# Gated MLP behind windowed attention on one core: 128 queries scored as two halves with 192 keys each, one tile for both heads' last blocks, P transposed by row halves

## The chip, the cores and the metric

The kernel runs on 1 core of one Trainium2 chip. The metric is device time in microseconds (us) of one execution. TensorE (PE; its weight loads are PEld), VectorE (DVE), ScalarE (ACT), GpSimd (POOL) and SyncE (SP) each work through their own queue in order and wait for one another by semaphores.

## The reference

There are 8 batches, 8 heads, 576 positions and a head size of 64. Attention looks back over a window of 128 positions, with a bias that falls with distance; a gated MLP follows, with a layer norm and a product along the sequence.

```python
scores = scale * np.matmul(q, k.transpose(0, 1, 3, 2))
slopes = 2.0 ** (-8.0 * (np.arange(H, dtype=np.float32) + 1) / H)
bias = slopes[:, None, None] * (-np.abs(rel).astype(np.float32))[None, :, :]
mask = (rel >= 0) & (rel < window)
scores = np.where(mask, scores + bias[None], -1000000000.0)
attn = np.exp(scores - np.max(scores, axis=-1, keepdims=True))
attn = attn / (np.sum(attn, axis=-1, keepdims=True) + 1e-09)
x = np.matmul(attn, v)                       # then heads side by side: (8, 576, 512)

h = np.maximum(x @ w_in, 0.0)                # 512 -> 1024
u, v = h[..., :512], h[..., 512:]
v_n = (v - mu) / np.sqrt(var + 1e-06)        # mean and variance over the 512
v_s = np.einsum('ts,bsd->btd', w_spatial, v_n) + b_spatial[None, :, None]
out = (u * v_s) @ w_out                      # 512 -> 512
```

## The kernel before

**Who sets the order.** Every step is handed to a planner (`Plan`) with its engine, an estimated cost, a due time and the buffers it reads and writes. `order` plays these through a list schedule (the ready step with the earliest due time goes first on its engine) and the steps are then written out in that order. Each engine's queue is therefore fixed at build time; semaphores enforce the data dependences at run time. `plan.buf(pool, tag, n, ...)` takes the next of `n` buffers that a tag cycles through, and a step on it depends on the users of the buffer that it replaces.

**The MLP.** For each batch `gated` runs five units on `v` (four `v_unit`, L711, and the remainder `v_rem`, L733), then eight `u_unit` (L763), eight `sp_unit` along the sequence (L784) and eight `o_unit` (L810). Every operand is kept as a high and a low part and multiplied in three passes, so a unit has 12 matmuls, `sp_unit` 14 and `v_rem` 8.

**Attention in the score way.** Heads go in pairs: there are four pairs (b, p) per batch. `scores` loads q, k and v, and `products` computes S = QK as 64-query blocks with at most 192 keys each (L527). The 64x64 products of both heads and both query halves are written into PSUM tiles of 128 queries by up to 256 keys. A tile t holds queries 128 t to 128 t + 127 and keys from 128 (t - 1) to the end of its queries, for one head: 128 columns for t = 0, 256 for t = 1 to 3, and 192 columns on 64 rows for t = 4. That is ten tiles per pair. Where a 64-query block does not reach, the table adds a large negative number. Tiles 0 to 3 of the two heads lie in the four banks tagged `s`; tile 4 of each head lies in the last 192 columns of the two banks x0 and x1 (tag `y`). For each tile VectorE adds the bias table and takes the minimum (L538), ScalarE takes exp and the row sum (L544), and after the sums' reciprocals ScalarE writes the scaled high part as fp16 into `pq` (L579) and VectorE the low part (L584). One DMA transpose per head turns all 18 blocks of 128 columns of `pq` into `pt` (L590), which has three half-pair buffers.

`attention` follows one pair later (`AHEAD = 1`). It scales and splits v (L602 to L633; a small DMA transpose at L613 spreads a maximum), multiplies V by the transposed P into x0 and x1, 288 queries in each (L646), and writes x with its low part (L655 on ScalarE, L659 on VectorE).

**Attention in the single-precision way.** At the start nothing else is ready, so `raw_tile` computes some pairs in plain fp32: scores (L444), table (L450), exp (L455), a transpose on TensorE (L473) and the product with v (L491). Before the change this holds for the four pairs of batch 0 and for pair (1,0). Only after that does `clear` zero the last columns of `pq` on POOL (L506).

**Preparation.** `split_w64` takes the weights, which arrive as 64-bit floats, apart into two parts. For `w_out` its staging buffers are those of `pt` and `vraw`, and the result has a place of its own.

**The queue of SP.** It issues every DMA: the loads of q and k (L423) and v (L425), the transposes (L590, L613), the weights and the stores (L820).

Of the kernel before, what the change touches and what calls it, by code (L numbers as in the profile page):

```python
# [44 lines left out]

class Plan:
# [94 lines left out]
def attn_gmlp_kernel(ctx, tc, qk, v, w_in, w_spT, b_sp, w_out, outT):  # L141
# [3 lines left out]
    nc = tc.nc  # L145
# [11 lines left out]
    VORDER = (0, 4, 1, 2, 3)  # L157

# [4 lines left out]
    WTMP, WST = ("vraw", 3), ("pt", 3)  # L163
# [21 lines left out]
    plan.kept["y"] = [x[:, 512 - 3 * D:].rearrange("p (a b) -> p a b", a=1) for x in plan.kept["x"]]  # L185
# [22 lines left out]
    ident = fixed([P, P], F32, "ident")  # L208
    powers = fixed([P, 2], F32, "powers")
    tabs = [fixed([P, 2 * P], BF16, f"tab{h}") for h in range(H)]  # L210
    win = fixed([P, NC_, 2, DF], F32R, "win")
    wout = fixed([P, ND, 2, DM], F32R, "wout")
# [4 lines left out]
    NB = 2 * NQ - 1  # L217
    OFF = [0] + [(2 * t - 1) * P for t in range(1, NQ)]
    prob = [fixed([P, NB * P], F32, f"prob{j}") for j in range(2)]
    pq = [fixed([P, 2, NB * P], F16, f"pq{j}") for j in range(2)]  # L220
    stat = [fixed([P, 4, 2, NQ], F32, f"stat{i}") for i in range(2)]
# [11 lines left out]
    maskt = plan.buf(work, "u", 7, [P, 2 * P], F32)  # L233
    minus = plan.buf(work, "u", 7, [P, P], F32R)

    def constants():
# [31 lines left out]
        for j in range(2):  # L268
            def f(j=j):
                nc.vector.memset(stat[j](), 1.0)  # L270
            plan.add("DVE", dve(64), 600, f, (), [(stat[j], x) for x in range(99)])
        for h in range(H):
            def f(h=h):
                slope = 2.0 ** (-8.0 * (h + 1) / H)
                nc.vector.scalar_tensor_tensor(tabs[h](), relf(), -8.0 * slope, maskt(), ALU.mult, ALU.add)
            plan.add("DVE", dve(256), 1000 + h * 4000, f, [(relf, 0), (maskt, 0)], [(tabs[h], 0)])
# [11 lines left out]
    def split_w64(src, dst, tmp, hi, lo, due, on_pe):  # L288
# [25 lines left out]
        copy(n, lambda: (hi(), x()), due + 3, [X], [HI], fast=True)  # L314
# [9 lines left out]
        if not on_pe:  # L324
            def f():
# [29 lines left out]
    def wout_weights(c, due):  # L355
        st = plan.buf(work, *WST, [P, DM, 2], I32)
# [4 lines left out]
        tmp = [plan.buf(work, *WTMP, [P, DM], F32) for _ in range(2)]  # L361
        split_w64((st, DM), (wout, (c,)), tmp, lambda: wout()[:, c, 0, :], lambda: wout()[:, c, 1, :], due, WPE[2])
# [67 lines left out]
    def raw_tile(b, p, t, raw, vr, xt, slot, due):  # L430
# [7 lines left out]
        pr = [lambda j=j: prob[j]()[:m, slot * 2 * P:slot * 2 * P + n] for j in range(2)]  # L438
        cols = [parts(prob[j], slot * 2 * P, slot * 2 * P + n) for j in range(2)]
# [6 lines left out]
        for j in range(2):  # L446
            h = 2 * p + j

            def f(j=j, h=h):
                nc.vector.tensor_tensor_reduce(pr[j](), sc[j]()[:m, 0, :n], tabs[h]()[:m, c0:c0 + n], -0.125, 3e38,  # L450
                                               ALU.add, ALU.min, st(NM, j))
            plan.add("DVE", dve(n), due + 300, f, [(sc[j], 0), (tabs[h], 0)], cols[j] + [(rstat, row)])
# [13 lines left out]
        tp = plan.buf(ps, *(("m", 2) if b == 0 else ("s", 4)), [P, 2, 2 * P], F32)  # L466
# [37 lines left out]
    def clear():  # L504
        for j in range(2):
            plan.add("POOL", 500, 0, lambda j=j: nc.gpsimd.memset(pq[j]()[:, :, OFF[NQ - 1]:], 0.0), (),  # L506
                     [k for a in range(2) for k in parts(pq[j], a * NB * P + OFF[NQ - 1], (a + 1) * NB * P)])


    BANKS = (((0, 1), ("s", 4)), ((2, 3), ("s", 4)), ((4,), ("y", 2)))  # L510

    WINDOWS = (((0, 0, 256, 0), (1, 256, 160, 128), (2, 512, 32, 256)),
               ((1, 416, 96, 0), (2, 544, 224, 0), (3, 768, 192, 96), (4, 1024, 64, 224)))

    def products(p, due, st, raw, RAWS, g, banks):

        SM, NM, RC, TM = range(4)
        sc = [[plan.buf(ps, *tag, [P, 2, 2 * P], F32) for _ in range(2)] for _, tag in banks]
        span = [(k, i, t, min(P, S - t * P), max(0, (t - 1) * P), min(S, (t + 1) * P)) for k, (ts_, _) in enumerate(banks) for i, t in enumerate(ts_)]

        def f():
            for k, i, t, m, k0, k1 in span:
                for q in range(t * P, t * P + m, D):
                    for j in range(2):
                        rows, out = slice(j * D, (j + 1) * D), slice(q - t * P, q - t * P + D)
                        a, z = max(k0, q - P), q + D
                        nc.tensor.matmul(sc[k][j]()[out, i, a - k0:z - k0], raw()[rows, 0, q:q + D], raw()[rows, 1, a:z],  # L527
                                         start=True, stop=True, skip_group_check=True)
        plan.add("PE", SWITCH + pe(*[4 * min(x[5] - x[4], 3 * D) for x in span]), due - 5000 + g * 3000, f, RAWS,
                 [(sc[k][j], i) for k, i, *_ in span for j in range(2)])  # L530
        for k, i, t, m, k0, k1 in span:
            for j in range(2):
                h, n, c0 = 2 * p + j, k1 - k0, P if t == 0 else 0
                pt = lambda j=j, m=m, t=t, n=n: prob[j]()[:m, OFF[t]:OFF[t] + n]
                d = due - 4500 + (t if len(banks) < 3 or t < NQ - 1 else -1) * 700 + j * 200

                def f(sc=sc[k][j], pt=pt, i=i, j=j, h=h, t=t, m=m, n=n, c0=c0):
                    nc.vector.tensor_tensor_reduce(pt(), sc()[:m, i, :n], tabs[h]()[:m, c0:c0 + n], -0.125, 3e38,  # L538
                                                   ALU.add, ALU.min, st()[:m, NM, j, t:t + 1])
                cols = parts(prob[j], OFF[t], OFF[t] + n)  # L540
                plan.add("DVE", dve(n), d, f, [(sc[k][j], i), (tabs[h], 0)], cols + [(st, (NM, j, t))])

                def f(pt=pt, j=j, t=t, m=m):
                    nc.scalar.activation(pt(), pt(), AF.Exp, bias=st()[:m, NM, j, t:t + 1], scale=-1.0,  # L544
                                         accum_out=st()[:m, SM, j, t:t + 1])
# [359 lines left out]
```

## Time and profile before

| | |
|---|---|
| time, median of three runs | 641.73 us (641.16 to 642.12) |
| span of the profiled execution | 640.1 us |
| PE busy | 598.2 us (93%), 5388 matmuls |
| PEld busy | 521.6 us (81%) |
| DVE busy | 533.7 us (83%) |
| ACT busy | 435.0 us (68%) |
| POOL busy | 30.4 us (5%) |
| DMA | 80.27 MB, 125 GB/s mean |

The profile shows one execution. Its own time is not listed apart from its span; the span runs from its first to its last instruction, and the three runs' median stands 1.6 us above it. Busy time of an engine counts overlapping instructions once. In a row of instruction groups the columns are the line of the kernel, the engine, the operation, the tiles (written <- read), their shapes, the count, then busy us, mean ns of one, and the idle time before them with the instruction that ended it. Matmuls overlap each other, so the mean of one is longer than the distance between two.

### The profile page before, as it was taken

How to read it: one execution, taken by the hardware profiler on the slowest of the kernel's cores; microseconds unless marked ns; L12 is line 12 of the kernel's file. 1: busy time of each engine (PE TensorE's matmuls, PEld its weight loads, DVE VectorE, ACT ScalarE, POOL GpSimd, SP SyncE). 2: the span in 40 equal slices, each digit the busy share in tenths (PEclk: the TensorE clock that was granted, in tenths of full speed). 3: DMA queues.
4: the chain of work that ended last, by engine and by line, in shares of the span. 5: the costliest groups of instructions: out<-in, count | busy, mean ns of one | idle time of the engine just before them, and what ended most of it. 6: DMA issues, size and time to landing. Idle time of an engine off the chain costs nothing. (4 is left out here: it accounts for less than half of the span.)

```text
span 640.1 us, 14937 instructions
## 1 busy us (share of the span) xinstructions
PE 598.2 (93%) x5388; PEld 521.6 (81%) x5388; DVE 533.7 (83%) x1953; ACT 435.0 (68%) x1324; POOL 30.4 (5%) x53
## 2 busy tenths in 40 slices
PE   4879899699999999999999999999999999999997
PEld 2445588588789978987789978998799878988997
DVE  7999898989997998889995999779979989873632
ACT  4697675897865887789762787667857987463211
POOL 1000010000100001000100001000100001000100
PEclk9997799899999999999999999999999999999999
DMA  7903123699456782498643774739567863433001
GB/s 265 335 19 99 47 67 102 145 219 183 123 135 134 142 203 54 112 187 213 142 95 80 172 171 98 120 112 200 90 129 168 151 134 65 78 73 77 0 19 57
DMA packets 153614, 80.27 MB, mean 125 GB/s; under 512 B 132930, under 2 KB 144194, under 8 KB 153540
## 3 DMA queue, kind: packets, MB, share of 16 engines
q1 hardware_dynamic: 153540, 79.32, 53.4%
q8 instruction: 42, 0.69, 0.5%
q14 instruction: 32, 0.26, 0.1%
HBM read 37.13 MB, written 9.44 MB: 73 GB/s over the span
## 5 line engine op out<-in xcount | busy, mean ns | idle before, releaser
L544 ACT ACTIVATE prob<-prob,stat 128x256 f32<-128x256 f32 (+2 forms) x270 | 126.0, 469 | 18.0 <-DVE stat L538 17.9
L784 PE MATMUL m<-wsp,vn 128*128 128x288 f32 x768 | 121.5, 297 | 2.7 <-ACT o L281 1.5
L810 PE MATMUL m<-gs,wout 128*128 128x288 f32 x768 | 111.5, 300 | 4.4 <-DVE u L792 1.6
L763 PE MATMUL m<-xt,win 128*128 128x288 f32 x768 | 112.0, 298 | 3.6 <-ACT u L285 1.8
L810 PEld LDWEIGHTS m<-gs,wout 128*128 128x128 f32 x768 | 103.5, 189 | 11.8 <-DVE u L792 2.5
L784 PEld LDWEIGHTS m<-wsp,vn 128*128 128x128 f32 x768 | 107.4, 188 | 6.2 <-ACT o L281 2.0
L763 PEld LDWEIGHTS m<-xt,win 128*128 128x128 f32 x768 | 104.0, 188 | 8.4 <-ACT u L285 3.0
L579 ACT ACTIVATE pq<-prob,stat 128x128 f16<-128x128 f32 x270 | 105.3, 467 | 4.6 <-DVE stat L567 2.0
L584 DVE SCALAR_TENSOR_TENSOR pq<-prob,stat,pq 128x128 f16<-128x128 f32 x270 | 105.8, 436 | 2.7 <-ACT pq L579 2.1
L711 PE MATMUL m<-win,xt 128*128 128x512 f32 x384 | 94.8, 400 | 3.4 <-ACT vt L285 1.9
L711 PEld LDWEIGHTS m<-win,xt 128*128 128x128 f32 x384 | 71.8, 191 | 23.9 <-ACT vt L285 4.1
L538 DVE CUSTOM_DVE_ANT_0 prob<-s,tab 128x256 f32<-128x256 f32 (+2 forms) x222 | 75.0, 380 | 0.3
L792 DVE TENSOR_TENSOR u<-m,u 128x288 f32<-128x288 f32 x64 | 28.6, 452 | 33.9 <-PE m L784 33.7
L681 POOL TENSOR_TENSOR st<-st,nhalf 128x1 f32<-128x1 f32 (+1 forms) x40 | 26.4, 660 | 553.3 <-DVE st L677 523.4
L544 ACT ACTIVATION_READ_ACCUMULATOR prob<-prob,stat 128x1 f32 (+1 forms) x270 | 51.4, 190 | 0.0
L285 ACT ACTIVATE u<-m 128x288 f32<-128x288 f32 x51 | 20.5, 406 | 45.2 <-PE m L763 45.0
L527 PE MATMUL s<-qkraw 64*64 64x192 f32 (+2 forms) x876 | 44.1, 318 | 6.8 <-DVE stat L538 6.8
L527 PEld LDWEIGHTS s<-qkraw 64*64 64x64 f32 x876 | 31.4, 136 | 13.2 <-DVE stat L538 9.7
L646 PE MATMUL x<-pt,vh 128*64 128x256 f16 (+6 forms) x756 | 41.8, 229 | 0.0
L646 PEld LDWEIGHTS <-vh 128*64 128x64 f16 x756 | 32.0, 110 | 5.6 <-issue 5.5
L281 ACT COPY o<-m 128x288 f32<-128x288 f32 x33 | 13.0, 395 | 33.8 <-PE m L810 32.2
L659 DVE SCALAR_TENSOR_TENSOR xt<-x,am,xt 128x288 fp32r<-128x288 f32 x54 | 25.6, 510 | 12.1 <-ACT xt L655 11.6
(134 smaller groups left out, 858.0 us busy)
## 6 DMA issues: line engine op xcount, KB each, us to landing
qkraw<-in_qk_dram SPq DMA_DIRECT2D x28, 576.0 KB, 4.5
out_dram<-o SPq DMA_DIRECT2D x64, 144.0 KB, 2.1
vraw<-in_v_dram SPq DMA_DIRECT2D x28, 320.0 KB, 3.0
vn<-in_w_in_dram SPq DMA_DIRECT2D x6, 512.0 KB, 6.3
pt<-in_w_out_dram SPq DMA_DIRECT2D x4, 512.0 KB, 4.1
gs<-in_w_spT_dram SPq DMA_DIRECT2D x4, 288.0 KB, 5.0
xt<-in_w_in_dram SPq DMA_DIRECT2D x2, 512.0 KB, 6.4
qkraw<-in_qk_dram SPq DMA_DIRECT2D x3, 320.0 KB, 8.6
```

The costliest lines, as they stand in the source:

```text
L527: nc.tensor.matmul(sc[k][j]()[out, i, a - k0:z - k0], raw()[rows, 0, q:q + D], raw()[rows, 1, a:z], start=True, stop=True, skip_group_chec ...
L538: nc.vector.tensor_tensor_reduce(pt(), sc()[:m, i, :n], tabs[h]()[:m, c0:c0 + n], -0.125, 3e38, ALU.add, ALU.min, st()[:m, NM, j, t:t + 1])
L544: nc.scalar.activation(pt(), pt(), AF.Exp, bias=st()[:m, NM, j, t:t + 1], scale=-1.0, accum_out=st()[:m, SM, j, t:t + 1])
L579: nc.scalar.activation(pq[j]()[:m, 0, cs], prob[j]()[:m, cs], AF.Copy, scale=st()[:m, RC, j, t:t + 1])
L584: nc.vector.scalar_tensor_tensor(pq[j]()[:m, 1, cs], prob[j]()[:m, cs], st()[:m, RC, j, t:t + 1], pq[j]()[:m, 0, cs], ALU.mult, ALU.subtract)
L646: nc.tensor.matmul(xp()[j * D:(j + 1) * D, x0:x0 + n], l()[:, kt, j * D:(j + 1) * D], rhs[:, o:o + n], start=j not in seen, stop=False, sk ...
L681: nc.gpsimd.tensor_tensor(st()[:m, 11:12], st()[:m, 10:11], nhalf()[:m], ALU.pow)
L711: nc.tensor.matmul(pt(), xt[c]()[:, X0[a] + t * P:X0[a] + (t + 1) * P], win()[:, c, w, DH:DF], start=(n == 0), stop=(n == 3 * NC_ - 1))
L763: nc.tensor.matmul(pt()[:, :HS], win()[:, c, w, d * P:(d + 1) * P], xt[c]()[:, X0[a] + hf * HS:X0[a] + (hf + 1) * HS], start=(n == 0), sto ...
L784: nc.tensor.matmul(pt()[:, :HS], l, r, start=(n == 0), stop=(n == len(ops) - 1))
L792: nc.vector.tensor_tensor(u(), pt()[:, :HS], u(), ALU.mult)
L810: nc.tensor.matmul(pt()[:, :HS], wout()[:, d, w, e * P:(e + 1) * P], gs[d]()[:, a, :], start=(n == 0), stop=(n == 3 * ND - 1))
```

## The change

Parts of the diff that only rename or pass arguments are left out.

- A score tile of 128 queries no longer spans 256 keys. Its two halves of 64 queries keep their own 192 keys in the same 192 columns, so tiles 1 to 3 have 192 columns instead of 256. The bias tables are cut to match (`tabs`), by copies from the full tables.
- The last 64 queries of both heads share one tile of 128 rows by 256 columns (`tabl` is its table), in the bank x0 alone; the two banks' other columns hold 256 and 320 queries of x instead of 288 each. Its products come first in `products`, and its tile comes last on VectorE. A pair has nine tiles.
- `prob`, `pq` and `stat` hold both heads in one buffer. In `pq` the halves lie at columns such that their keys line up when rows 0 to 63 are transposed from 64 columns further on than rows 64 to 127. So each head has two transposes of 64 rows, of 14 blocks of 128 columns for the first head and of 18 for the second, which has the shared tile. `pt` has two buffers for a whole pair.
- All of `pq` is cleared once on POOL. Pair (1,0) goes the score way; only batch 0 keeps the single-precision way, with its buffers placed in the ones that are used later (`told`, `more`, `raw3`).
- `w_out` is staged in the place where its result goes, so the high part is written after the last read of the staging.

```diff
-    WTMP, WST = ("vraw", 3), ("pt", 3)
+    WTMP = ("vraw", 3)
-    WHOLE = 2
-    RAW = {(0, p) for p in range(4)} | {(1, p) for p in range(1)}
...
-    plan.kept["y"] = [x[:, 512 - 3 * D:].rearrange("p (a b) -> p a b", a=1) for x in plan.kept["x"]]
+    plan.kept["y"] = [plan.kept["x"][0][:, 2 * P:]]
...
+    def tables():
+        plan.add("POOL", 700, 60000, lambda: nc.gpsimd.memset(tabl(), MASKED), (), [(tabl, 0), (tabl, 1)])
+        ...
+                nc.sync.dma_start(tabs()[rows], told()[rows, :, cs])
+            plan.add("SP", 800, 60000, f, heads, [(tabs, i)])
+            ...
+                nc.sync.dma_start(tabl()[rows, :, (1 - i) * D:(1 - i) * D + W], src[:, :, i, cs])
+            plan.add("SP", 800, 60000, f, heads, [(tabl, i)])
...
     def wout_weights(c, due):
-        st = plan.buf(work, *WST, [P, DM, 2], I32)
+        st = plan.buf(work, f"wout{c}", 1, [P, DM, 2], I32)
...
     def clear():
-        for j in range(2):
-            plan.add("POOL", 500, 0, lambda j=j: nc.gpsimd.memset(pq[j]()[:, :, OFF[NQ - 1]:], 0.0), (),
+        plan.add("POOL", 2500, 0, lambda: nc.gpsimd.memset(pq(), 0.0), (), parts(pq, 0, PQ, 64))
...
-    BANKS = (((0, 1), ("s", 4)), ((2, 3), ("s", 4)), ((4,), ("y", 2)))
+    def pieces(p):
+        out = []
+        for j in range(2):
+            for t in range(NQ - 1):
+                n = T0 if t == 0 else W
+                out.append((2 * j + (t == 3), (2 * W, 0, W, 0)[t], n, j * HEAD + (0 if t == 0 else T0 + (t - 1) * W),
+                            BASE[j] + (0 if t == 0 else T0 + (t - 1) * 2 * P + D), PLANE[j], lambda h=2 * p + j, n=n: tabs()[:, h, W - n:]))
+        out.append((4, 0, 2 * P, 2 * HEAD, BASE[1] + PLANE[0], PLANE[1], lambda: tabl()[:, p, :]))
+        return out
...
-            for k, i, t, m, k0, k1 in span:
-                for q in range(t * P, t * P + m, D):
+            for j in range(2):
+                one(4, (1 - j) * D, j, j, 2 * NQ - 2, (2 * NQ - 4) * D)
+            for t in range(NQ - 1):
+                for half in range(2):
                     for j in range(2):
-                        rows, out = slice(j * D, (j + 1) * D), slice(q - t * P, q - t * P + D)
-                        a, z = max(k0, q - P), q + D
-                        nc.tensor.matmul(sc[k][j]()[out, i, a - k0:z - k0], raw()[rows, 0, q:q + D], raw()[rows, 1, a:z],
-                                         start=True, stop=True, skip_group_check=True)
+                        i = 2 * t + half
+                        one(tiles[j * (NQ - 1) + t][0], tiles[j * (NQ - 1) + t][1], j, half, i, (i - 2) * D + (D if t == 0 else 0))
...
-            pts.append(plan.buf(work, "pt", 3, [P, 2 * NB, P], F16))
-                nc.sync.dma_start_transpose(out=pts[j](), in_=pq[j]().rearrange("p a b -> p (a b)"))
-            plan.add("SP", 3400, d + 1500, f, parts(pq[j], 0, 2 * NB * P), [(pts[j], 0)])
+            nb = 2 * PLANE[j] // P
+            for half in range(2):
+                c0 = BASE[j] + (1 - half) * D
+                ...
+                    rows = slice(half * D, (half + 1) * D)
+                    nc.sync.dma_start_transpose(out=pts()[:, BLOCK[j]:BLOCK[j] + nb, rows], in_=pq()[rows, c0:c0 + nb * P])
+                plan.add("SP", 1700, d + 1500 + half, f, parts(pq, c0, c0 + nb * P, 64), [(pts, (j, half))])
...
-            qs = slice(hf * HS, (hf + 1) * HS)
+            q0, q1 = (0, QSPLIT) if hf == 0 else (QSPLIT, S)
```

More of the change, by code (lines that the diff above doesn't have):

```diff
@@ L72, in either @@
         deps, starts = set(), set()
+        reads, writes = ([(b.of, (b.key, part)) if isinstance(b, Sub) else (b, part) for b, part in x] for x in (reads, writes))
         for b, part in reads:
@@ L207, in attn_gmlp_kernel @@
     nhalf = fixed([P, 1], F32, "nhalf")
-    ident = fixed([P, P], F32, "ident")
     powers = fixed([P, 2], F32, "powers")
-    tabs = [fixed([P, 2 * P], BF16, f"tab{h}") for h in range(H)]
+    tabs = fixed([P, H, W], BF16, "tabs")
+    tabl = fixed([P, NP, 2 * P], BF16, "tabl")
     win = fixed([P, NC_, 2, DF], F32R, "win")
-    wout = fixed([P, ND, 2, DM], F32R, "wout")
+    wout = {}
     wsp = fixed([P, NQ - 1, 2, S], F32R, "wsp")
@@ L216, in attn_gmlp_kernel @@
     l2 = fixed([P, DH], F32R, "l2")
[L217 to L221, printed above, removed]
+    NT = 2 * (NQ - 1) + 1
+    prob = fixed([P, 2 * HEAD + 2 * P], F32, "prob")
+    PLANE = [7 * P, 9 * P]
+    BASE = [0, 2 * PLANE[0] + D]
+    BLOCK = [0, 14]
+    PQ = BASE[1] + 2 * PLANE[1] + D
+    pq = fixed([P, PQ], F16, "pq")
+    stat = [fixed([P, 4, NT], F32, f"stat{i}") for i in range(2)]
     rstat = fixed([P, 8, 8], F32, "rstat")
@@ L233, in attn_gmlp_kernel @@
     maskt = plan.buf(work, "u", 7, [P, 2 * P], F32)
+    ident = plan.buf(work, "u", 7, [P, P], F32)
     minus = plan.buf(work, "u", 7, [P, P], F32R)
+    pt_raw, pt_tab = (plan.buf(work, "pt", 2, [P, 2048], F32) for _ in range(2))
+    raw3 = Sub(pt_raw, "raw", lambda x: x[:, :2 * S].rearrange("p (a s) -> p a s", a=2))
+    vr3 = Sub(pt_raw, "v", lambda x: x[:, 2 * S:2 * S + NQ * P].rearrange("p (t n) -> p t n", t=NQ))
+    told = Sub(pt_tab, "tab", lambda x: x[:, :H * P].bitcast(BF16).rearrange("p (h n) -> p h n", h=H))
+    more = Sub(pt_tab, "prob", lambda x: x[:, H * P:H * P + 4 * P])
     def constants():
@@ L413, in tail, with load @@
         copy(R, lambda: (xt()[:, S:S + R], xt()[:, 2 * S:2 * S + R]), due, xcols(xt, 1, (NQ - 1) * P, S), [(xt, 2)], fast=True)
-    def load(b, p, due, pieces, qtag=("qkraw", 3), vtag=("vraw", 3)):
-        raw = plan.buf(work, *qtag, [P, 2, S], F32)
-        vr = plan.buf(work, *vtag, [P, NQ, P], F32)
+    def load(b, p, due, pieces, raw=None, vr=None):
+        raw = raw or plan.buf(work, "qkraw", 3, [P, 2, S], F32)
+        vr = vr or plan.buf(work, "vraw", 3, [P, NQ, P], F32)
         src = qk[b, 2 * p:2 * p + 2].rearrange("h d a s -> (h d) a s")
@@ L437, in raw_tile @@
         sc = [plan.buf(ps, "s", 4, [P, 2, 2 * P], F32) for _ in range(2)]
-        pr = [lambda j=j: prob[j]()[:m, slot * 2 * P:slot * 2 * P + n] for j in range(2)]
-        cols = [parts(prob[j], slot * 2 * P, slot * 2 * P + n) for j in range(2)]
+        area, a0 = (prob, slot * 4 * P) if slot < 3 else (more, 0)
+        pr = [lambda j=j: area()[:m, a0 + j * 2 * P:a0 + j * 2 * P + n] for j in range(2)]
+        cols = [parts(area, a0 + j * 2 * P, a0 + j * 2 * P + n, 64) for j in range(2)]
         def f():
@@ L554, in scores @@
         RAWS, VRS = [(raw, t) for t in range(NQ)], [(vr, t) for t in range(NQ)]
[L555 to L562 removed]
+        products(p, due, st, raw, RAWS, (b, p) == (1, 0))
@@ L563, in scores @@
+        pts = plan.buf(work, "pt", 2, [P, 32, P], F16)
+        tiles = pieces(p)
         for j in range(2):
             d = due + j * 1500
[L566 to L572 removed]
@@ L833, in gated @@
             {"u": u_unit, "s": sp_unit, "o": o_unit}[kind](*todo[kind].pop(0))
+    loads = [load(0, p, [-50000 + 1000 * p, -20000 + 1000 * p], [2, NQ], *((raw3, vr3) if p == 3 else ())) for p in range(NP)]
     constants()
+    tables()
     for c in range(NC_):
@@ L842, in attn_gmlp_kernel @@
         wsp_weights(c, FIRST + 8000 + 2000 * c)
-    where = [(("qkraw", 3), ("vraw", 3))] * 3 + [(("pt", 3), ("pt", 3))]
     x0 = [plan.buf(work, "xt", 6, [P, 2 * S + R], F32R) for _ in range(NP)]
-    loads = [load(0, p, [-50000 + 1000 * p, -20000 + 1000 * p], [2, NQ], *where[p]) for p in range(NP)]
     def first(t):
```

172 lines of the change are left out of this document (95 added, 77 removed).

## The prediction, before the changed kernel was run

> **What bounds the kernel now.** I read the page's shares first, then a table of stages cut at the start of each batch's L733 matmuls, then the chain that ended last.
>
> ```profile
> PE 598.2 (93%) x5388; PEld 521.6 (81%) x5388; DVE 533.7 (83%) x1953; ACT 435.0 (68%) x1324; POOL 30.4 (5%) x53
> PE 19%; DVE 9%; ACT 3%; DMA 1%; issue 1%; POOL 0%; ACTq 0%; POOLq 0%
> PE m L810 6%; PE m L784 5%; PE m L763 4%; DVE pq L584 2%; PE m L711 2%; DVE prob L538 1%; ACT prob L544 1%; PE x L646 1%; PE s L527 1%; DVE st L672 1%; ACT pq L579 1%; DMA out_dram<-o 1%; DVE xt L659 1%; DVE vt L685 1%; DVE u L792 0%
> ```
> TensorE looks like the bound, but VectorE is close behind and holds a third of the chain. How much of TensorE's time is work that no other engine can shorten is read from the stages. Columns: stage, its length, busy us and instructions of PE, PEld, DVE, ACT, POOL, then the granted clock.
>
> ```profile
> 87.10:162.40 75.30, 68.86 (x687) 60.66 (x686) 67.95 (x255) 57.49 (x179) 2.51 (x4) 0.95 0.62 144
> 162.40:232.50 70.10, 68.51 (x673) 61.94 (x672) 62.54 (x231) 53.17 (x165) 2.89 (x5) 1.00 0.63 139
> 232.50:307.10 74.60, 71.63 (x709) 63.44 (x708) 68.08 (x266) 59.11 (x191) 3.28 (x5) 1.00 0.70 149
> 307.10:375.70 68.60, 66.19 (x638) 60.60 (x637) 58.43 (x204) 45.27 (x135) 2.94 (x5) 1.00 0.55 127
> 375.70:447.50 71.80, 68.68 (x674) 61.88 (x673) 62.63 (x230) 51.87 (x161) 3.82 (x5) 1.00 0.64 137
> 447.50:520.30 72.80, 69.51 (x674) 61.98 (x673) 64.90 (x254) 57.84 (x187) 3.29 (x5) 1.00 0.69 140
> 520.30:585.90 65.60, 64.42 (x601) 59.29 (x600) 49.07 (x165) 38.41 (x108) 3.88 (x5) 1.00 0.38 82
> 585.90:640.10 54.20, 50.86 (x349) 48.57 (x347) 22.64 (x55) 10.76 (x23) 2.83 (x5) 1.00 0.07 23
> 581.63 1.51 PE x L646 x42
> 583.13 2.96 PE m L711 x12
> 443.13 1.35 PE s L527 x28
> 444.49 0.23 PE x L527 x4
> ```
> The last stage has no attention in it. Its 50.86 us of PE and the one L711 unit just before it (2.96) are a batch's dense products: 53.8 us. One pair of heads adds 1.51 for its products with P (L646) and 1.35 + 0.23 = 1.58 for its scores (L527). A batch issues 360 matmuls of its own, four attentions 168, each scores 36, so the instruction counts give the scores in a stage: 4, 5, 3, 4, 4, 2 in the second to seventh. Dense PE time is 53.8 + 6.04 + 1.58 n: 66.2, 67.7, 64.6, 66.2, 66.2, 63.0. The stage is longer than that by 3.9, 6.9, 4.0, 5.6, 6.6 and 2.6 us. VectorE's busy time as a share of the dense time is 0.945, 1.005, 0.905, 0.946, 0.980, 0.779. The stall follows VectorE's load almost in order: little at 0.78, four at 0.91, nearly seven at 1.0. So about 30 us of these six stages, and some 6 of the first, is TensorE waiting on work that a lighter VectorE and ScalarE would deliver sooner.
>
> **The change, part by part.** *Fewer and narrower score tiles.* A pair had ten tiles: two of 128 columns, six of 256, two of 192 on 64 rows. It gets nine: two of 128, six of 192, one of 256. Per operation that removes five of 256 and adds four of 192; I assume that 128 rows cost what 64 do.
>
> ```profile
> L544 ACT ACTIVATE prob<-prob,stat 128x256 f32<-128x256 f32 x162 | 80.6, 501 | 2.1 <-DVE stat L538 2.1
> L544 ACT ACTIVATE prob<-prob,stat 64x192 f32<-64x192 f32 x54 | 24.2, 449 | 13.7 <-DVE stat L538 13.7
> L579 ACT ACTIVATE pq<-prob,stat 128x256 f16<-128x256 f32 x162 | 70.8, 497 | 0.0
> L579 ACT ACTIVATE pq<-prob,stat 64x192 f16<-64x192 f32 x54 | 24.0, 445 | 0.0
> L584 DVE SCALAR_TENSOR_TENSOR pq<-prob,stat,pq 128x256 f16<-128x256 f32 x162 | 71.2, 478 | 0.5
> L584 DVE SCALAR_TENSOR_TENSOR pq<-prob,stat,pq 64x192 f16<-64x192 f32 x54 | 21.9, 406 | 0.0
> L538 DVE CUSTOM_DVE_ANT_0 prob<-s,tab 128x256 f32<-128x256 f32 x162 | 60.9, 413 | 0.0
> L538 DVE CUSTOM_DVE_ANT_0 prob<-x,tab 64x192 f32<-64x192 f32 x48 | 15.5, 345 | 9.2 <-PE x L527 9.2
> ```
> Instructions overlap, so I use busy time over count. Exp: 5 x 0.498 - 4 x 0.448 = 0.70 us. Scaled copy: 5 x 0.437 - 4 x 0.444 = 0.41. Low part (L584): 5 x 0.440 - 4 x 0.406 = 0.58. Scores with table (L538): 5 x 0.376 - 4 x 0.323 = 0.59. ScalarE loses 1.1 us and VectorE 1.17 us per pair.
>
> What of it reaches the end, from two sides. The chain's first piece is this:
>
> ```profile
> 425.75 1.99 ACT prob L544 x8
> ```
>  By the stages: with VectorE less 1.17 n, the shares become 0.875, 0.92, 0.85, 0.876, 0.91, 0.742; read off the same curve the stalls are 3.7, 4.3, 3.4, 3.7, 4.1, 2.2, a gain of 8.2 us, and with the mean of it for the first stage 9.6. By the chain: its whole shares of the 640.1 us are 2% for L584 and 1% each for L538, L544 and L579, 12.8, 6.4, 6.4 and 6.4 us; cut by the share each operation loses (14%, 17%, 15%, 10%) that is 4.5 us. It is followed back only to that piece at 426 us; by the counts above some 7.5 of 27 pairs lie behind it (4, 2 and a third of 4), so 16 us in all. I take 12, near the middle: a shorter chain hands over to the next one. TensorE's own products are the same in number and width.
>
> *Pair (1,0) leaves the single-precision way (L430 to L502).*
>
> ```profile
> L444 PE MATMUL s<-qkraw 64*128 64x256 f32 x48 | 10.3, 483 | 0.2 <-DVE rstat L450 0.2
> L473 PE MATMUL s<-ident,prob 128*128 128x128 f32 x14 | 2.5, 301 | 1.0 <-DVE prob L464 1.0
> L491 PE MATMUL x<-pq,vraw 128*64 128x128 f32 x112 | 8.5, 283 | 2.4 <-DVE pq L281 2.3
> 126.65 2.96 PE L527 MATMUL s<-qkraw 64*64 64x64 f32 x32 [1.39 <-DVE stat L538]
> ```
> Twelve of the 48, all 14 and 28 of the 112 are its own: 2.6 + 2.5 + 2.1 = 7.2 us of PE, against 3.1 for a pair in the new way, so 4.1 less. But TensorE waits for VectorE right behind it (last row), where the time may be lost again: 0 to 4.1, I take 2. The first stage also shows a clock of 0.95, 3.8 us lost; if the waits shrink part of it may come back: 0 to 3.8, I take 1.
>
> *Four transposes by row halves for two.* A pair's two of 18 blocks of 128 columns on 128 rows become two of 14 and two of 18 on 64 rows, all on SP's queue.
>
> ```profile
> L590 SPq DMA_TRANSPOSE pt<-pq x54: 2377/2782/5570, 121.4 to 575.2; - x54
> L613 SPq DMA_TRANSPOSE vl<-vl x27: 1106/1174/2214, 110.4 to 553.1; - x27
> pt<-pq SPq DMA_TRANSPOSE x54, 4.8
> vl<-vl SPq DMA_TRANSPOSE x27, 2.3
> 121.45 6.12 SPq L590 DMA_TRANSPOSE pt<-pq  x2
> 133.12 0.41 PE L646 MATMUL x<-pt,vh 128*64 128x256 f16 x4
> 572.22 5.70 SPq L590 DMA_TRANSPOSE pt<-pq  x2
> ```
> The trace has 18 blocks (2.78 us to issue, 4.8 to landing) and one (1.17 and 2.3), so about 0.095 us of issue per full block. If cost goes by area, 14 and 18 half blocks take 1.74 and 1.93, 7.3 us a pair for 5.6, and the last landing comes 0.6 us later. If it goes by column blocks alone, they take 2.4 and 2.78, 10.4 us a pair, and the second head's landing comes 2.8 us later. Attention starts between 0.4 and 6.3 us after the second transpose's landing in the 27 pairs (4.4 in the first, 1.6 in the last: second issue plus 4.8, against 133.12 and 581.63). A delay of 2.8 exceeds that room in twelve of them, by 12.0 us together; one of 0.6 in two, by 0.4. I take 1, nearer the area end, because the two issue rows differ by less than three times for 18 times the area. What queues behind these issues on SP (L423, L425 loads, L820 stores) has its due times far ahead or nobody waiting. A lower end below nothing exists too: whole buffers for two pairs replace three half ones, so a second head need not wait for the attention before; no row shows that wait ending last.
>
> The Trainium skill ("DMA: Bandwidth & Descriptors", section "Rules for kernel authors") advises against two transfers to disjoint partition halves, since both use the same 16 engines and serialize. By that rule the split brings no speed and leaves the extra issues, which is the upper case of 12 us; no row of before shows a transpose of 64 rows. The rule has its rival below.
>
> *One-time work.* Clearing all of pq (4224 columns) for 2 x 512:
>
> ```profile
> L506 POOL MEMSET pq<- x2: 529/530/532, 109.3 to 109.8; 128x512 f16 x2
> 83.88 0.72 POOL L681 TENSOR_TENSOR st<-st,nhalf 128x1 f32<-128x1 f32 x1 [12.90 <-DVE xt L499]
> 91.69 5.07 PE L763 MATMUL m<-xt,win 128*128 128x288 f32 x36
> ```
> At 0.53 per 512 it is 4.4 us on POOL, ready when the last single-precision products of batch 0 are done, at about 82 us; the layer norm's power (L681) queued behind it can slip by 0 to 2.5 us. I take nothing: TensorE has the u products (L763) to do meanwhile, and if that cover were gone the 2.5 us would be paid once. The four table copies and their fill, the one VectorE fill of masked columns, the identity moved to a shared buffer, w_out's own staging and the high part written later all lie before 110 us beside a busy VectorE: under 1 us, taken as nothing.
>
> *Order in the last block.* Its products now come first in the scores and its tile last on VectorE, in x0 alone.
>
> ```profile
> ACT xt L655 <- PE x L527: 8.6, 7, 2.8
> 510.90 0.41 PE L646 MATMUL x<-pt,vh 128*64 128x256 f16 x4
> ```
> Seven times L655, which reads other columns of the same bank, waited until the last-block products behind the attention were done. That wait shrinks, off the chain mostly; what may replace it is a rival.
>
> Sum against the profiled span of 640.1: -12 - 2 - 1 + 1 = -14, 626.1. The three runs' median of 641.73 is 1.6 above this span, so 627.7; I say 628.
>
> **The rivals.** *Transposes late.* If a 64-row issue costs as much as a 128-row one, attention comes late by 12 us as above, and where both heads are ready together the first head's two issues delay the second's by as much again: 628 + 12 to 24, say 645. It decides from 14 us on. For it: the room of 0.4 to 6.3; against: the one-block row at 1.17.
>
> *A bank wait on the last tile.* L646 writes x0 beside the last-block scores. If it must wait for the tile that is now ninth on VectorE, 2.8 us after the first, every attention that starts within about 4.2 us of the scores pays up to 2.8. Seven of 27 do (in the first the scores end at 129.6 and L646 starts at 133.12; in the last of them it starts at 510.90): 20 us, 648. For it: the seven bank waits; against: the written order may put L646 ahead of that tile.
>
> *Nothing gained.* The stalls come from the order and not from load; only 1 or 2 us remain: 641.
>
> *More gained.* All stages fall to the 2.6 us of the lightest, and the first follows: 30 - 16 = 14 from six stages, 3 from the first, 4 and 4 from the start: 641.7 - 25 + 1 = 618, at best 608 with waits nearly gone.
>
> **How the numbers follow.** Forecast with its neighbourhood (620 to 637) 0.52; more gained 0.19; nothing gained 0.12, half of it within 0.2%; transposes late 0.10; bank wait 0.07. 0.2% of 641.7 is 1.3 us, about what a measurement of this kernel tells from no change. Faster by more: 0.52 + 0.19 + 0.04 + a little of the late cases, 0.77; same 0.07; slower 0.16. The range, 608 to 643, leaves out most of the late cases and little below; the forecast's own range is 614 to 639.
>
> **What would show it.** Right: VectorE about 32 and ScalarE about 30 us less busy, stages of 66 to 71 us, scores' and attention's matmuls unchanged in time, the single-precision products gone after 85 us. Wrong: L646 with idle time before it, ended by a transpose or by the score operation on VectorE; SP issues of over 2.2 us; stages as long as before with VectorE below 0.9 of dense time.

## The result, and the profile after

The changed kernel takes 650.09 us (median of four runs, 648.23 to 653.09); the kernel before took 641.44 us (641.08 to 642.12) beside it. The ratio is 1.0141, interval 1.0113 to 1.0169: 8.6 us slower, where 13.7 us faster was forecast and the range ended at 643. The profiled execution after has a span of 648.2 us.

The line numbers move with the change: scores' matmuls L578 (before L527), scores with table L594 (L538), exp L599 (L544), high part L628 (L579), low part L633 (L584), transposes L642 (L590), small transpose L665 (L613), attention's matmuls L701 (L646), x L712 and L716 (L655, L659), `v_rem` L790 (L733), output units L867 (L810), stores L877 (L820); the output copies are a helper's line, L314 (L281).

The shares of the page after: the work did become less.

```profile
PE 592.7 (91%) x5392; PEld 520.3 (80%) x5392; DVE 517.1 (80%) x1913; ACT 379.8 (59%) x1200; POOL 33.2 (5%) x53
```

TensorE is 5.5 us less busy, VectorE 16.6 and ScalarE 55.2, and the span is 8.1 longer. The groups by shape, after, show the narrower tiles at their expected price.

```profile
L599 ACT ACTIVATE prob<-prob,stat 128x192 f32<-128x192 f32 x168 | 74.0, 442 | 0.4 <-DVE stat L594 0.4
L628 ACT ACTIVATE pq<-prob,stat 128x192 f16<-128x192 f32 x168 | 64.7, 443 | 0.0
L633 DVE SCALAR_TENSOR_TENSOR pq<-prob,stat,pq 128x192 f16<-128x192 f32 x168 | 62.4, 410 | 0.0
L594 DVE CUSTOM_DVE_ANT_0 prob<-s,tabs 128x192 f32<-128x192 f32 x168 | 50.7, 353 | 0.1
```

The five full stages behind the first, with the same columns and cuts as before (each batch's `v_rem`):

```profile
161.70:236.70 75.00, 69.73 (x674) 62.27 (x673) 61.36 (x236) 46.28 (x152) 3.06 (x5) 1.00 0.64 131
236.70:310.60 73.90, 70.11 (x674) 63.52 (x673) 60.40 (x230) 45.76 (x152) 3.33 (x5) 0.98 0.66 131
310.60:383.00 72.40, 68.50 (x673) 62.45 (x672) 59.34 (x223) 42.44 (x139) 3.33 (x5) 1.00 0.59 125
383.00:455.20 72.20, 68.44 (x673) 62.41 (x672) 59.94 (x227) 44.16 (x146) 3.33 (x5) 1.00 0.64 129
455.20:526.90 71.70, 68.54 (x674) 62.61 (x673) 59.94 (x227) 44.25 (x146) 3.33 (x5) 1.00 0.63 128
```

The first of them begins where it did (161.7 against 162.4), so the start is not where the time went. The five take 71.7 to 75.0 us. With four pairs' scores each, a stage's dense work is 66.2 us by the prediction's count, so TensorE still loses 5.5 to 9 us in each, though VectorE is at 0.90 to 0.93 of the dense time, a load at which the kernel before lost about 4. The loss is no longer VectorE's load. The waits of after and of before say what came instead (line, what it waited for, us in total, times, longest). TensorE's weight loads (PEld) and its matmuls (PE) wait at the same places, so their two rows are not added up:

```profile
DVE am L670 <- DMA vl<-vl: 16.3, 14, 2.1
...
PEld x L578 <- DVE xt L716: 12.9, 5, 3.3
PE x L578 <- DVE xt L716: 11.8, 5, 3.1
...
DVE o L314 <- DMA out_dram<-o: 8.5, 5, 2.6
...
PEld L701 <- DMA pt<-pq: 4.2, 5, 1.6
...
ACT o L314 <- DMA out_dram<-o: 3.1, 3, 2.0
```

```profile
DVE am L618 <- DMA vl<-vl: 1.7, 3, 0.7
...
ACT o L281 <- DMA out_dram<-o: 1.5, 2, 1.3
...
DVE o L281 <- DMA out_dram<-o: 0.8, 1, 0.8
```

Two kinds of wait are new. One is for DMAs on SP's queue: VectorE for the small transpose that spreads v's maximum, the output copies for a buffer `o` whose store has not landed, and attention for its transposes. The other is TensorE's scores waiting until x has been read out of the shared bank x0. The timeline shows how one such place looks:

```profile
377.14 0.40 ACT L314 COPY o<-m 128x288 f32<-128x288 f32 x1 [2.02 <-DMA out_dram<-o]
...
377.95 0.97 DVE L716 SCALAR_TENSOR_TENSOR xt<-x,am,xt 128x256 fp32r<-128x256 f32 x2 [2.20 <-ACT xt L712]
...
378.49 0.38 PE L578 MATMUL x<-qkraw 64*64 64x192 f32 x2 [3.06 <-DVE xt L716]
```

Read from the bottom: the last block's products, now first in the scores, wait 3.06 us for VectorE's x; that waits for ScalarE's; and ScalarE had stood 2.02 us at an output copy whose buffer a store still held. Bank and queue meet in one chain, and the experiments had to take them apart. The transposes themselves, the big one and the small one:

```profile
L642 SPq DMA_TRANSPOSE pt<-pq x112: 1234/1640/4089, 95.4 to 570.6; - x112
L665 SPq DMA_TRANSPOSE vl<-vl x28: 1112/1516/2532, 120.8 to 560.7; - x28
```

Four issues at 1.64 us are 6.6 us a pair, against 5.6 for two at 2.78. The small transpose, whose shape did not change, went from 1.17 to 1.52 us to issue.

### The profile page after: what moved, and what is told of

It is laid out like the page before. It is cut to its first block, busy times and chain, and to the rows that moved or that the text cites. A ratio compares the mean times of both kernels' runs of the same rounds, so it can differ in the third digit from the quotient of the medians.

```text
span 648.2 us, 14898 instructions
## 1 busy us (share of the span) xinstructions
PE 592.7 (91%) x5392; PEld 520.3 (80%) x5392; DVE 517.1 (80%) x1913; ACT 379.8 (59%) x1200; POOL 33.2 (5%) x53
## 5 line engine op out<-in xcount | busy, mean ns | idle before, releaser
L599 ACT ACTIVATE prob<-prob,stat 128x192 f32<-128x192 f32 (+2 forms) x252 | 109.7, 437 | 28.6 <-DVE stat L594 28.5
L820 PE MATMUL m<-xt,win 128*128 128x288 f32 x768 | 111.7, 298 | 6.0 <-ACT u L318 1.8
L628 ACT ACTIVATE pq<-prob,stat 128x192 f16<-128x192 f32 (+2 forms) x252 | 92.4, 439 | 37.9 <-issue 24.7
L867 PE MATMUL m<-gs,wout 128*128 128x288 f32 x768 | 111.1, 299 | 2.2 <-DVE u L319 1.4
L820 PEld LDWEIGHTS m<-xt,win 128*128 128x128 f32 x768 | 103.8, 188 | 11.2 <-ACT u L318 3.8
L867 PEld LDWEIGHTS m<-gs,wout 128*128 128x128 f32 x768 | 103.8, 188 | 6.8 <-DVE u L319 1.7
L633 DVE SCALAR_TENSOR_TENSOR pq<-prob,stat,pq 128x192 f16<-128x192 f32 (+2 forms) x252 | 90.8, 404 | 2.0 <-ACT pq L628 1.9
L594 DVE CUSTOM_DVE_ANT_0 prob<-s,tabs 128x128 f32<-128x128 f32 (+1 forms) x224 | 62.9, 336 | 1.4 <-PE s L578 1.3
L578 PE MATMUL s<-qkraw 64*64 64x192 f32 (+2 forms) x896 | 50.5, 319 | 0.0
L599 ACT ACTIVATION_READ_ACCUMULATOR prob<-prob,stat 128x1 f32 x252 | 47.3, 188 | 0.0
L701 PE MATMUL x<-pt,vh 128*64 128x128 f16 (+2 forms) x784 | 43.8, 230 | 3.2 <-DMA pt<-pq 3.2
L701 PEld LDWEIGHTS <-vh 128*64 128x64 f16 x784 | 35.0, 110 | 10.1 <-issue 5.5
L314 ACT COPY o<-m 128x288 f32<-128x288 f32 x28 | 11.2, 400 | 51.1 <-PE m L867 46.8
L578 PEld LDWEIGHTS s<-qkraw 64*64 64x64 f32 x896 | 39.2, 137 | 0.9
L701 PE MATMUL x<-pt,vl 128*64 128x256 f16 x392 | 35.7, 228 | 0.9 <-DVE vl L685 0.9
```

The source lines that it names most:

```text
L578: nc.tensor.matmul(flat(k)[half * D:(half + 1) * D, c0 + a - back:c0 + z - back], raw()[j * D:(j + 1) * D, 0, i * D:z], raw()[j * D:(j + 1 ...
L594: nc.vector.tensor_tensor_reduce(pt(), flat(bank)[:, c0:c0 + n], tab(), -0.125, 3e38, ALU.add, ALU.min, st()[:, NM, k:k + 1])
L599: nc.scalar.activation(pt(), pt(), AF.Exp, bias=st()[:, NM, k:k + 1], scale=-1.0, accum_out=st()[:, SM, k:k + 1])
L628: nc.scalar.activation(pq()[:, qc:qc + n], prob()[:, pc:pc + n], AF.Copy, scale=st()[:, RC, k:k + 1])
L633: nc.vector.scalar_tensor_tensor(pq()[:, qc + plane:qc + plane + n], prob()[:, pc:pc + n], st()[:, RC, k:k + 1], pq()[:, qc:qc + n], ALU.m ...
L701: nc.tensor.matmul(xp()[j * D:(j + 1) * D, x0:x0 + w], l()[:, kt, j * D:(j + 1) * D], pts().rearrange("p a b -> p (a b)")[:, c:c + w], sta ...
```

## The experiments

Four explanations stood against one another: that the transposes by row halves cost more than their area; that it is their number; that the scores in the bank x0 wait for x; and that the planner, with other costs and buffers, wrote out a worse order. Unless a text says otherwise, a kernel is the changed one with the edit shown; every comparison with the kernel before was made on the same chip. The kernel before took 641.4 to 641.8 us beside each of them, so their times are also set against one another.

**The last block's products back at the end of the scores.**

```diff
-            for j in range(2):
-                one(4, (1 - j) * D, j, j, 2 * NQ - 2, (2 * NQ - 4) * D)
             for t in range(NQ - 1):
                 ...
+            for j in range(2):
+                one(4, (1 - j) * D, j, j, 2 * NQ - 2, (2 * NQ - 4) * D)
```

> The changed kernel with the last block's products put back to the end of the scores step; nothing else. Theory B (bank): the changed kernel's loss is TensorE waiting, at the head of the scores, until VectorE has read x out of the same bank x0 (24.7 us in ten waits, 0.4 us before). The 1.4 us of other products then run ahead of the wait, so ten waits shrink by up to 1.4 us each: 640 to 645 us, the wait at 10 to 15 us. Theory S (SP queue): four transposes per pair make the small transposes and the stores late, and that is the loss; the order in the scores changes nothing: 648 to 652 us.

Measured: 649.31 us (646.9 to 651.81), ratio 1.0126 (1.0092 to 1.0159). TensorE's waits for x in the bank fell from 11.8 us to 4.0, at five places both times, and the time did not follow. (The 24.7 us in ten waits of the expectation count each of the five places twice, once for its weight load and once for its matmul.)

```profile
PEld x L578 <- DVE xt L716: 5.7, 5, 1.4
...
PE x L578 <- DVE xt L716: 4.0, 5, 1.1
```

**The last block in free columns of the score banks**, so that scores and x share no bank. The second head's last block is left out of the computation here.

```diff
-        out.append((4, 0, 2 * P, ...
+        out.append((1, W, 2 * P, ...
...
-        sc = [... for _ in range(4)] + [plan.buf(ps, "y", 1, [P, 2 * P], F32)]
+        sc = [... for _ in range(4)]
...
-                one(4, (1 - j) * D, j, j, ...
+                one(1 + 2 * j, W + (1 - j) * D, j, j, ...
```

> The changed kernel with the last blocks' products written to free columns of two score banks instead of x0; the tile of 128 rows is still read as one, from the first of these banks, so the second head's last block is not in it (its result is left out). Same instructions and sizes, no bank shared between scores and x. Theory B: the waits of the scores on the reading of x are gone, 24.7 us to near 1, and 630 to 640 us follow. Theory S: TensorE then waits somewhere else for the same late x, 646 to 650 us.

Measured: 645.69 us (644.83 to 647.69), ratio 1.0078 (1.0055 to 1.01). The bank wait is gone, and 4.4 us with it. The waits for DMAs stayed:

```profile
DVE am L670 <- DMA vl<-vl: 16.0, 13, 2.0
...
DVE o L314 <- DMA out_dram<-o: 11.7, 8, 2.1
```

So the bank is worth a few microseconds at most, and the kernel is still slower than before without it.

**One transpose of 128 rows per head**, 14 and 18 blocks, from the same `pq`. The shift by 64 columns that lines the halves' keys up is left out, so rows 64 to 127 hand attention other keys.

```diff
-            for half in range(2):
-                c0 = BASE[j] + (1 - half) * D
-                ...
-                    nc.sync.dma_start_transpose(out=pts()[:, BLOCK[j]:BLOCK[j] + nb, rows], in_=pq()[rows, c0:c0 + nb * P])
-                plan.add("SP", 1700, ...
+                nc.sync.dma_start_transpose(out=pts()[:, BLOCK[j]:BLOCK[j] + nb, :], in_=pq()[:, BASE[j]:BASE[j] + nb * P])
+            plan.add("SP", 3400, ...
```

> The changed kernel with one transpose of 128 rows per head (14 and 18 blocks of 128 columns) instead of two of 64 rows, so the keys of one query half stand in wrong places (the alignment is left out). SP issues two big transposes per pair again. Theory S: small transposes and stores are on time, VectorE's wait for the small transpose falls from 16.3 us to under 5, and 638 to 643 us follow. Theory B: little, 646 to 650 us.

Measured: **624.94 us** (624.65 to 626.19), ratio 0.9749 (0.9734 to 0.9764), 25.2 us below the changed kernel. Its page, its transposes and what is left of the waits:

```profile
PE 587.0 (94%) x5392; PEld 518.9 (83%) x5392; DVE 516.0 (83%) x1913; ACT 378.3 (61%) x1200; POOL 33.2 (5%) x53
```

```profile
L638 SPq DMA_TRANSPOSE pt<-pq x56: 1367/2632/5294, 93.8 to 544.4; - x56
```

```profile
DVE am L666 <- DMA vl<-vl: 4.3, 4, 1.5
...
DVE o L314 <- DMA out_dram<-o: 2.2, 3, 0.8
```

VectorE and ScalarE do what they did in the changed kernel (516.0 and 378.3 us); the bank x0 is still shared. Only the transposes differ. The planner wrote out the same order again: the instructions of VectorE, ScalarE and POOL, the steps of TensorE and the DMAs on SP follow one another in this trace as in that of the changed kernel.

**The kernel before with each transpose cut by row halves**, nothing else changed.

```diff
-            def f(j=j):
-                nc.sync.dma_start_transpose(out=pts[j](), in_=pq[j]()...)
-            plan.add("SP", 3400, ...
+            for half in range(2):
+                def f(j=j, rows=slice(half * D, (half + 1) * D)):
+                    nc.sync.dma_start_transpose(out=pts[j]()[:, :, rows], in_=pq[j]()[rows]...)
+                plan.add("SP", 1700, ...
```

> The kernel before with each transpose of 18 blocks cut into two of 64 rows; same result, same layout, nothing else. Theory S: it loses as the changed kernel does, 647 to 652 us. Theory B: the room of 0.4 to 6.3 us before attention takes most of it, 641 to 644 us. The issue of one transpose of 18 blocks on 64 rows should show about 1.65 us.

Measured: 661.1 us (658.61 to 662.94), ratio 1.0307 (1.0278 to 1.0335): 19.5 us from this part alone, and here too the order in the trace is that of the kernel before. One issue took 2.00 us (median), not 1.65. The same waits appear:

```profile
DVE am L619 <- DMA vl<-vl: 12.2, 10, 2.8
PEld L647 <- DMA pt<-pq: 8.2, 9, 2.1
DVE o L281 <- DMA out_dram<-o: 7.1, 7, 1.8
```

The first four runs settle which part of the change costs the time, and that the planner's order is not what costs it, since the order is the same with and without the row halves. They leave open whether it is the rows or the number of issues, and how it reaches TensorE.

**The small transpose left out** (each row then uses its own maximum, so the spreading of v's maximum over the rows is not computed).

```diff
-            nc.sync.dma_start_transpose(out=wide(1), in_=wide(0))
-        plan.add("SP", 300, d + 2, f, [(vl, 0)], [(vl, 1)])
```

> The changed kernel with the small transpose of the maximum left out (each row of v is scaled by its own value instead of the common one); the VectorE steps on it stay. Four transposes of 64 rows per pair as in the changed kernel. Theory S1 (the loss runs through the small transpose, queued behind the big ones: VectorE waits 16.3 us for it): 630 to 638 us. Theory S2 (the loss is P itself landing late, or all of SP's queue): 643 to 649 us.

Measured: 638.67 us (637.64 to 642.49), ratio 0.9953 (0.9937 to 0.997), 11.4 below the changed kernel. Taken alone that looks like the wait of VectorE for this transpose; the control below takes the reading away.

**The stores issued by GpSimd** instead of SP.

```diff
-                nc.sync.dma_start(outT[...], o())
-            plan.add("SP", dma(P * HS * 4), due, f, [(o, 0)], ())
+                nc.gpsimd.dma_start(outT[...], o())
+            plan.add("POOL", 1000, due, f, [(o, 0)], ())
```

> The changed kernel with its 64 stores issued by GpSimd instead of SyncE; nothing else. Theory S3 (stores queued behind the four transposes hold the output buffers: ScalarE and VectorE wait 11.6 us for them): 636 to 643 us. Theories S1 and S2: 645 to 650 us.

Measured: 659.45 us (656.99 to 661.92), ratio 1.0274 (1.0238 to 1.0311). The run says nothing on SP's queue, because the planner's order changed with it. POOL now stands still until the copy of each store is done, but the layer norm's power, which it also computes, was hardly waited for (0.7 us). What made this run slow is not shown.

```profile
POOL out_dram L877 <- ACT o L314: 232.1, 22, 26.9
...
DVE vt L742 <- POOL st L738: 0.7, 2, 0.5
```

**The planner told that a transpose of 64 rows costs 2600 ns** instead of 1700; the work stays the same, only the order changes (the planner also moves a few steps between VectorE and ScalarE).

```diff
-                plan.add("SP", 1700, d + 1500 + half, ...
+                plan.add("SP", 2600, d + 1500 + half, ...
```

> The changed kernel with the planner's cost of a transpose of 64 rows at 2600 instead of 1700, so that it plans attention later and puts other products ahead of it; the chip's work is the same, only its order differs. If TensorE loses because the order expects P too early: 638 to 645 us. If SP and the DMA engines simply take too long: 648 to 655 us.

Measured: 644.98 us (642.96 to 648.3), ratio 1.0052 (1.0035 to 1.0069). That is 5.1 below the changed kernel. The waits for DMAs nearly go: VectorE's for the small transpose falls from 16.3 to 1.7 us in all, the output copies' for stores from 11.6 to 2.4. Yet the kernel stays 20 us above the one with whole transposes. An order that leaves the late transposes room avoids the waits and still loses most of the time; where in that order TensorE loses it is not shown.

**Another layout without the shift.** A tile holds the same 64 queries of both heads, one head on each half of the rows, the sides swapped for odd blocks. Nine tiles (64, 128 and seven of 192 columns) lie in the four score banks, so the bank x0 is free of scores, and both heads' P is turned by two transposes of 128 rows and 16 blocks.

```diff
-            for half in range(2):
-                ...
-                    nc.sync.dma_start_transpose(out=pts()[:, BLOCK[j]:BLOCK[j] + nb, rows], in_=pq()[rows, c0:c0 + nb * P])
+            def f(j=j):
+                nc.sync.dma_start_transpose(out=pts()[:, 16 * j:16 * j + 16, :], in_=pq()[:, 2 * PLANE * j:2 * PLANE * (j + 1)])
```

> A tile holds the same 64 queries of both heads (one head per row half, swapped for odd blocks), so both halves have the same keys: nine tiles of 64, 128 and seven times 192 columns, all in the four score banks, and the transposes are two of 128 rows and 16 blocks again. The result is complete. Theory S: as the kernel with whole transposes (624.9 us) or a little better, 615 to 626 us, since 128 fewer columns go through VectorE and ScalarE per pair and no bank is shared with x. If instead the narrower tiles were not what helped there: 640 us.

Measured: 625.04 us (624.13 to 627.2), ratio 0.9748 (0.9721 to 0.9775). The next two cut these transposes in two, once by columns and once by rows. Both have four issues a pair, of the same area, with the same cost for the planner, and the order of all instructions on PE, VectorE, ScalarE and POOL is the same in both, and the same as without the cut.

```diff
 by columns: four of 128 rows and 8 blocks
+                    b0 = 16 * j + 8 * half
+                    nc.sync.dma_start_transpose(out=pts()[:, b0:b0 + 8, :], in_=pq()[:, b0 * P:(b0 + 8) * P])
 by rows: four of 64 rows and 16 blocks
+                    nc.sync.dma_start_transpose(out=pts()[:, 16 * j:16 * j + 16, rows], in_=pq()[rows, 2 * PLANE * j:2 * PLANE * (j + 1)])
```

> The kernel with tiles of both heads' same queries, each transpose cut in two by columns: four of 128 rows and 8 blocks per pair, issued after the same steps; the result is complete. Theory R (rows: it is the 64-row form that takes longer per packet, 27 to 29 ns against 24): 625 to 632 us. Theory C (count: two more issues with their fixed part of 1.1 us each are the cost): 640 to 650 us.

> The same kernel, each transpose cut in two by rows: four of 64 rows and 16 blocks; the result is complete. Both theories: 640 to 650 us, as the kernel before lost 19.5 us by the same cut. If it stays under 632 the cut costs only where the planned order is tight. The packets tell R from C: under R their mean is 27 to 29 ns here and 24 ns in the cut by columns.

Measured: by columns **624.42 us** (623.51 to 625.83), ratio 0.974 (0.9724 to 0.9756); by rows **638.49 us** (634.86 to 642.5), ratio 0.9954 (0.9928 to 0.9981). Twice the issues cost nothing when they are cut by columns, and 14.1 us when they are cut by rows. The sign of theory R came too: the transposes' packets, 118272 of 256 bytes in each trace, took 25.6 ns on average by columns and 29.3 by rows. The DMA queue (packets, MB, share of 16 engines) and the transposes, by columns first:

```profile
q1 hardware_dynamic: 146916, 77.27, 55.3%
```

```profile
L623 SPq DMA_TRANSPOSE pt<-pq x112: 1231/1287/3307, 90.9 to 556.2; - x112
```

and by rows:

```profile
q1 hardware_dynamic: 146916, 77.27, 58.7%
```

```profile
L622 SPq DMA_TRANSPOSE pt<-pq x112: 1242/1792/3289, 93.2 to 569.3; - x112
```

Because the order is the same, the two traces can be laid on each other, matmul by matmul. The second trace falls behind by 0.9 us up to 210 us of the first, 3.0 at 240, 6.4 at 300, 9.1 at 390, 10.6 at 450 and 11.4 at the end. (Both profiles are of the fastest execution, 623.51 and 634.86 us, so they show 11.4 of the 14.1 us between the medians.) The largest single step, 1.7 us, is at the first `v` unit of a batch. SP's queue ahead of it and the output copy that lets it start, by columns:

```profile
210.15 5.39 SPq L623 DMA_TRANSPOSE pt<-pq  x4
215.64 1.18 SPq L646 DMA_TRANSPOSE vl<-vl  x1
216.91 0.53 SPq L455 DMA_DIRECT2D qkraw<-in_qk_dram  x1
218.68 1.92 SPq L857 DMA_DIRECT2D out_dram<-o  x2
...
223.64 0.40 ACT L307 COPY o<-m 128x288 f32<-128x288 f32 x1 [1.85 <-DMA out_dram<-o]
```

and by rows:

```profile
211.99 6.98 SPq L622 DMA_TRANSPOSE pt<-pq  x4
219.08 1.70 SPq L645 DMA_TRANSPOSE vl<-vl  x1
220.87 1.61 SPq L455 DMA_DIRECT2D qkraw<-in_qk_dram  x1
222.58 0.86 SPq L856 DMA_DIRECT2D out_dram<-o  x2
...
226.94 0.40 ACT L307 COPY o<-m 128x288 f32<-128x288 f32 x1 [4.22 <-DMA out_dram<-o]
...
227.39 0.97 PE L747 MATMUL m<-win,xt 128*128 128x512 f32 x3 [1.56 <-ACT o L307]
```

From the first transpose to the stores it is 8.53 us by columns and 10.59 by rows: 1.6 more in the four transposes, 0.5 in the small one and 1.1 in the load behind it, less what the queue had to wait for by columns. The stores go out later, the copy waits 4.22 us instead of 1.85, and TensorE stands 1.56 us. Three more steps, 2.4 us together, are attention's matmuls waiting for a transpose directly. At the others ScalarE or VectorE was late. Those of over 0.3 us can be followed back in the same way, wait by wait: six, 3.8 us together, lead to a store or a small transpose for which an engine waits longer than by columns, one of 0.65 us to a part of `pq` that its transpose still held, and one of 0.7 us to no DMA. The remaining 2 us are smaller steps. The waits for DMAs in all say the same, by columns:

```profile
DVE am L651 <- DMA vl<-vl: 3.2, 3, 1.9
...
DVE o L307 <- DMA out_dram<-o: 2.9, 2, 1.8
...
ACT o L307 <- DMA out_dram<-o: 1.9, 1, 1.9
```

and by rows:

```profile
DVE am L650 <- DMA vl<-vl: 13.3, 10, 3.6
...
ACT o L307 <- DMA out_dram<-o: 9.1, 5, 4.2
...
ACT pq L612 <- DMA pt<-pq: 4.9, 4, 2.1
...
DVE o L307 <- DMA out_dram<-o: 3.3, 2, 1.9
...
PE x L681 <- DMA pt<-pq: 1.9, 3, 0.9
```

One thing stays open: a transpose of 64 rows also writes 64 columns of each block of `pt` instead of 128. No run tells whether the fewer rows read or the narrower pieces written make its packets slower.

**Two controls on the small transpose**: left out of the kernel before, and left out of the changed kernel together with the cost of 2600 (the same part of the computation is missing as above).

> Control for the leaving out of the small transpose, on the kernel before (each row of v scaled by its own value). Theory S1: there VectorE waits only 1.7 us for it, so 637 to 642 us, and the 11.4 us gained on the changed kernel belong to the split. If it gains about 10 us here too, S1 has no support from that run.

> The changed kernel with the small transpose left out and the planner's cost of a 64-row transpose at 2600. If the two paths (small transpose behind the big ones, attention planned before P is there) are separate, their gains of 11.4 and 5.1 us add to 631 to 636 us. If one is the other in disguise: 637 to 640 us.

Measured: the first 649.56 us (648.7 to 650.74), ratio 1.0126 (1.0108 to 1.0143), which is 8 us slower with less work, as neither case of the expectation had it. The second 637.18 us (636.88 to 639.21), ratio 0.9938 (0.992 to 0.9956), only 1.5 below the small transpose left out alone, where separate gains would have added to 16.5. Leaving out a step gives the planner another order, and with it this kernel moved by 8 us the wrong way. The 11.4 of the small transpose is therefore no evidence on how much of the loss its wait carries. The three pairs that differ in the row halves (25.2, 19.5 and 14.1 us; the first also in the shift) are free of this, because the order is the same within each.

## Why the prediction was wrong, step by step

- *The failed step* is "Four transposes by row halves for two", taken at +1 us. It measured 25.2 on the changed kernel, 19.5 on the kernel before and 14.1 on the other layout, each time with the order unchanged. With 25 in its place, the prediction's sum is 626.1 - 1 + 25 + 1.6 = 652; measured 650.1.
- *Why it failed is not the price of an issue.* That came near the area end, as chosen: 6.6 us a pair by the medians, where area gave 7.3. What failed is the sentence on the cover, that what queues behind the issues on SP "has its due times far ahead or nobody waiting". It names the loads and the stores and leaves out the small transpose. Output copies do wait for the stores to free their buffers `o` (2.3 us in all before, 11.6 after), and VectorE waits for the small transpose (1.7 before, 16.3 after; 3.2 by columns and 13.3 by rows). The prediction priced only attention's own room of 0.4 to 6.3 us behind the transposes. In the pair by columns and by rows, attention and its buffers make about 3 of the 11.4 us and the stores and small transposes about 5.5.
- *The rule of the Trainium skill* ("DMA: Bandwidth & Descriptors", section "Rules for kernel authors"), that transfers to disjoint partition halves serialize and one of 128 partitions should be used, pointed the right way, and by it the upper case of 12 should have been weighed more. But standing one behind another is not what costs here: the four transposes cut by columns do so too (5.39 us for four at the place shown), and cost nothing (624.4 against 625.0).
- *The rival "transposes late"* gave 645 and came true on the side and nearly in size, by another way: its price of 10.4 us of issue a pair didn't occur.
- *The rival "bank wait on the last tile"* put the wait at attention's matmuls. The wait that appeared was the reverse, the next scores waiting for x in that bank, and moving it away brought 0.8 us (within the spread) and 4.4.
- *Narrower tiles*: right. Busy time over count came to 0.440, 0.385, 0.371 and 0.302 us for the four operations on 192 columns, where 0.448, 0.444, 0.406 and 0.323 were taken from 64 rows. VectorE and ScalarE together lost 72 us, forecast 62; the 72 also holds what pair (1,0) no longer does in single precision. How it is shared came out otherwise, 16.6 and 55.2 for 32 and 30, since the planner may give a copy to either engine and gave more of them to VectorE.
- *What of it reaches the end* (12), the pair (1,0) (2) and the clock (1) can't be separated, but their sum can be read from the kernel with whole transposes: 641.6 to 624.9 is 16.6 us, against 15 in the prediction's sum without transposes. That the sum fits does not show that each term did.
- *One-time work*: the clearing of `pq` took 3.6 us on POOL where 4.4 was expected; the second stage started 0.7 us earlier than before, so nothing of it shows.
- *A misreading without effect*: VectorE's part of the chain was 9 of the 33 points, a little over a quarter and not a third. No number of the sum hangs on it.

The forecast of 628 was thus close to the change without its row halves, for which 624.9 was measured.

## What to carry to other kernels

When a DMA is split or grows on a queue that stores and small transfers share, list every consumer of what is issued behind it, buffers that a store must free included, and price the delay at each; the room of the transposes' own reader is not the bound. Cut a DMA transpose by columns rather than by rows, and choose a layout whose transposes take all 128 rows: the version by columns takes 624.4 us, 2.6% below the kernel before (ratio 0.974, 0.9724 to 0.9756). Where a planner sets the order, compare the order in the two traces before an effect is read from a run. Where it is the same, as in the three pairs here, the difference is the edit's. Where it is not, run the same edit on the kernel before: leaving the small transpose out made that one 8 us slower, though the work became less.

## What the runs showed of the hardware

- A transpose of 64 rows by 16 blocks of 128 columns takes 1.79 us to issue (median) and 4.4 to landing; one of 128 rows by 8 blocks, the same number of elements, takes 1.29 and 3.6.
- With the same 146916 packets and 77.27 MB, the 16 DMA engines were busy 55.3% of 621.8 us by columns and 58.7% of 633.2 us by rows: 343.9 and 371.7 us each, 8% more for the same bytes. All of the difference lies in the transposes' packets of 256 bytes (25.6 and 29.3 ns each, 188.9 and 216.9 us for each engine).
- A transpose of 16 blocks on 128 rows takes 2.55 us to issue (median), one of 8 blocks 1.29. All issues together take 143 us of SP with two of 16 blocks a pair and 163 us with four of 8, so the cut by columns is not free on SP, though it cost the kernel no time; by rows it is 192 us.
- What stands behind the 64-row transposes on SP can take longer to issue as well, at the place shown 1.70 us for 1.18 and 1.61 for 0.53, though its shape is the same. Over all 28 small transposes the median stays 1.13 us and the mean goes from 1.16 to 1.35.
